# RetNet attention and a Swish MLP in one kernel: batch 1's queries loaded in two spans, the first MLP weights in half rows, the first up products in pairs

## The chip, the cores and the metric

The kernel runs on one core of one Trainium2 chip. The metric is the time of one execution on the device in microseconds (us): 311.66 us as the median of three runs (311.6 to 312.2). The profile is of one further execution. The engines are called as the profile calls them: PE multiplies matrices, DVE and POOL work elementwise, ACT does activations and copies, SP issues DMAs. PEld is PE's loading of the stationary operand, which lies beside its matmuls.

## The reference

`q`, `k` and `v` have 8 batches, 8 heads, 576 positions and 64 values per head. The output has 4608 rows of 512 values. Cut to what is computed:

```python
scores = scale * np.matmul(q, k.transpose(0, 1, 3, 2))
Dmat = np.where(rel >= 0, gamma[:, None, None] ** rel[None, :, :], 0.0)   # rel = i - j
attn_out = np.matmul(scores * Dmat[None], v)
x = attn_out.transpose(0, 2, 1, 3).reshape(B * S, H * D)                  # 4608 x 512
h = x @ w_in                                                              # 512 x 2048
g = h * (1.0 / (1.0 + np.exp(-beta * h)))
out = g @ w_out                                                           # 2048 x 512
```

There is no softmax: a fixed decay per head takes its place. So attention can be done in chunks of positions that hand on a state, the sum of keys times values.

## The kernel before, in words

**Work.** Each batch has 512 main positions in four chunks of 128; the last 64 positions of all batches are packed in a ninth block. Items of attention have a number i: i = 0 to 3 are the chunks of batch 0, 4 to 7 those of batch 1, 8 to 11 those of batch 2. For a chunk, keys become bf16 (`pre`, POOL), are turned by PE (`t_k`, four transposes, copied from PSUM by ACT, L304) and multiplied with the turned queries (`a_sc`); DVE multiplies the scores with the causal mask into `R` (L333, two products a chunk). `a_O` multiplies `R` with the values, `a_cross` adds queries times state, `a_x` copies the result into `xT`, the MLP's input (L380 to L384). `a_st` updates the state in PSUM and ACT copies it in two halves (L401), into `sbd`, or into `end` after the last chunk.

**Queries.** `pre_q` multiplies a batch's queries with gains (L247), `t_q` turns them in two groups of eight transposes (L297, L298). Before the change a batch's queries are laid out four positions to a partition, so every transpose needs all of the batch.

**MLP.** A block of 512 positions has 16 ups and 16 downs. An up (`up`, L406) is four matmuls, one for each quarter `ko` of the 512 inputs, into one of three PSUM tiles of the tag "mm", and a Silu on ACT (L415). A down is four matmuls of 512 columns (L426); four of them fill one output tile, which DVE copies (L433) and SP stores (L436).

**Order.** The order is written by hand. Batch 0's attention stands first, line by line (L457 to L497). Then `merged` goes through a list `fill` of MLP steps: 16 ups of batch 0 (steps 0 to 15), 16 downs (16 to 31, `d0` = 16), then batch 1 (`u1` = 32): ten ups of its first two chunks, ten of its last two, six whole ups, 16 downs, and so on. `streams` holds everything else with a key: a piece goes ahead of the first step whose number is not below its key. Each engine runs its instructions in this program order, so an instruction that waits holds up all that follows on its engine. At the same key order, `second` is `a_O`, `a_cross`, `a_x` of two chunks and the state of the second.

**Weights.** `w_in` comes through four staging tiles (tag "wt") and is cast to bf16 by DVE and POOL (L186). `w_out` comes through the same tiles, so its loads (L190) wait for these casts; it is scaled by DVE and ACT (L198, L200). SP issues nearly all DMAs in program order: batch 0's queries, keys and values, the pieces of `w_in`, those of `w_out`, then batch 1's queries, keys and values. A new load waits for one some eight places ahead of it, whose semaphore it takes.

Of the kernel before, what the change touches and what calls it, by code (L numbers as in the profile page):

```python
# [19 lines left out]
def kernel(  # L20
# [15 lines left out]
    P = 128  # L36
# [34 lines left out]
    QB = 2  # L71
    q_tiles, kv_tiles = {}, {}

    def load_q(b):
# [3 lines left out]
        t = stage.tile([P, H, CB, D], F32, name="qn", tag="qn", bufs=2)  # L78
        for u in range(2):
            w = slice(u * HP, (u + 1) * HP)  # L80
            nc.sync.dma_start(t[:, w].rearrange("p h i d -> p h (i d)"),
                              q[b, w, :MB, :].rearrange("h (p i) d -> p h (i d)", i=CB))
# [38 lines left out]
    pos = consts.tile([P, 2, CB + 1], F32, name="pos")  # L121
    for j, (step, mul) in enumerate(((1, CB), (P, 1))):
        nc.gpsimd.iota(pos[:, j, :CB], pattern=[[step, CB]], base=0, channel_multiplier=mul,
                       allow_small_or_imprecise_dtypes=True)
        for x in range(2):
            nc.gpsimd.iota(pos[x * TL:(x + 1) * TL, j, CB:], pattern=[[0, 1]], base=MB, channel_multiplier=1,
                           allow_small_or_imprecise_dtypes=True)
    lscale = consts.tile([P, 1], F32, name="lscale")
    nc.vector.memset(lscale[:], math.log(scale))
    lg = consts.tile([P, 2, CB + 1, H], F32, name="lg")  # L130
    for h in range(H):
        nc.vector.tensor_scalar(lg[:, :, :, h], pos[:], math.log(1.0 - 2.0 ** (-5.0 - h)), None, ALU.mult)
    gq = consts.tile([P, CB + 1, H], F32, name="gq")
    gv = consts.tile([P, CB + 1, H], F32, name="gv")
    nc.scalar.activation(gq[:], lg[:, 0], ACT.Exp, bias=lscale[:])
    nc.scalar.activation(gv[:], lg[:, 1], ACT.Exp, scale=-1.0)
# [11 lines left out]
    causal4 = consts.tile([P, HP, P], BF16, name="causal4")  # L148
    nc.gpsimd.tensor_copy(causal4[:], causal[:].unsqueeze(1).to_broadcast([P, HP, P]))
# [17 lines left out]
    pieces = [(f, 256) for f in range(0, 1024, 256)] + [(f, 512) for f in range(1024, d_ff, 512)]  # L167
# [5 lines left out]
    def load_w_in(g):  # L173
# [4 lines left out]
        nc.sync.dma_start(t, w_in_r[:, :, f0:f0 + fn])  # L178
        wts[g] = t

    def cast_w_in(g, kos=range(KO)):
        t = wts[g]
        f0, fn = pieces[g]
        for ko in kos:
            on_pool = ko == KO - 1 or g < 4 and ko > 1
            (nc.gpsimd if on_pool else nc.vector).tensor_copy(w_in_sb[:, ko, f0:f0 + fn], t[:, ko])  # L186
# [50 lines left out]
    def pre_q(b, n):  # L237
# [4 lines left out]
        if b < 2:  # L242
            hs, cs = slice(n // 2 * HP, (n // 2 + 1) * HP), slice(n % 2 * 2, n % 2 * 2 + 2)
            e = nc.vector
        else:
            hs, cs, e = slice(0, H), slice(n, n + 1), nc.gpsimd
        e.tensor_tensor(batch[b]["qs"][:, cs, hs], q_tiles[b][:, hs, cs].rearrange("p h i d -> p i h d"),  # L247
                        gq[:, cs, hs].unsqueeze(3).to_broadcast([P, cs.stop - cs.start, hs.stop - hs.start, D]),
# [50 lines left out]

    def t_k(i):  # L300
# [320 lines left out]
```

## Time and profile before

| what | value |
|---|---|
| median of three runs | 311.66 us |
| profiled execution | 311.92 us |
| its span, first to last instruction | 310.1 us |
| granted TensorE clock | 0.998 |
| first up of batch 0 | 19.48 us |
| first down of batch 0 | 34.12 us |
| first half up of batch 1 | 52.22 us |
| first down of batch 1 | 71.54 us |
| moved by DMA | 52.79 MB, 149 GB/s of HBM traffic over the span |

The page lists busy times of the engines, the span in 40 slices, the chain of work that ended last, and groups of instructions by line, with the time that their engine idled before them and what ended it. The timeline lists instructions in order of time: start, length, engine, line, operation, tiles, shape, number, and in brackets the idle time before and its releaser. Several alike are merged into one row, "x6". A busy time of PE counts a matmul from its start to the end of its pipeline, so waits on PE are read from the distances of starts. SPq and ACTq are the sequencers that issue DMAs.

### The profile page before, as it was taken

What the parts mean: (1) busy time and instruction counts of PE and PEld (TensorE: products, weight loads), DVE (VectorE), ACT (ScalarE), POOL (GpSimd) and SP (SyncE); (2) the same over time, 40 slices, a digit from 0 to 9 for tenths busy, and PEclk for the clock granted to TensorE, in tenths of its full rate; (3) what the DMA queues carried; (4) which work ended last, traced back from release to release, by engine and by line L of the source; (5) the groups of instructions that cost most, each with busy time, mean ns of one, the idle gap of its engine ahead of it and who ended that gap; (6) DMA issues with size and microseconds to landing.
All of it is one profiled execution on the core that took longest, in us unless ns stands there. A gap on an engine that the chain in (4) does not pass through costs nothing.

```text
span 310.1 us, 5363 instructions
## 1 busy us (share of the span) xinstructions
PE 298.5 (96%) x2144; PEld 157.8 (51%) x2177; DVE 106.9 (34%) x191; ACT 143.0 (46%) x256; POOL 96.0 (31%) x131
## 2 busy tenths in 40 slices
PE   7789999999999999999999999999999999999995
PEld 5544456775544454454554545455545444444444
DVE  7554476342531342434430434043405420010012
ACT  5567626995138412560186117711673037207700
POOL 4663026846524282254308031902420000000000
PEclk9999999999999999999999999999999999999999
DMA  8999999998989999999897697968852110031011
GB/s 207 221 355 387 380 232 273 233 257 179 202 197 162 224 189 235 218 212 198 133 234 107 136 205 207 201 115 192 196 76 37 68 70 0 17 88 34 0 70 68
DMA packets 123897, 52.79 MB, mean 170 GB/s; under 512 B 105680, under 2 KB 116320, under 8 KB 123872
## 3 DMA queue, kind: packets, MB, share of 16 engines
q1 hardware_dynamic: 98496, 46.15, 61.5%
q10 hardware_dynamic: 25376, 6.30, 13.6%
q8 instruction: 17, 0.28, 0.4%
q14 instruction: 8, 0.07, 0.1%
HBM read 36.71 MB, written 9.44 MB: 149 GB/s over the span
## 4 chain that ended last, share of the span: by engine, by line
PE 85%; DMA 6%; SPq 5%; DVE 1%; issue 1%; ACT 1%; POOL 1%; POOLq 0%
PE po L426 40%; PE ph L413 35%; DMA wt<-in_moe_w_in_dram 4%; SPq L94 3%; PE O L366 3%; PE sc L323 3%; DMA qn<-in_q_dram 2%; PE O L351 2%; PE st L396 2%; SPq L178 1%; POOL qs L247 1%; PE T L297 1%; PE T L303 1%; ACT gT L415 0%; DVE xT L384 0%
## 5 line engine op out<-in xcount | busy, mean ns | idle before, releaser
L415 ACT ACTIVATE gT<-ph,beta_sb 128x512 bf16<-128x512 f32 (+1 forms) x154 | 99.2, 659 | 86.3 <-PE ph L413 83.4
L413 PE MATMUL ph<-xT,w_in_sb 128*128 128x512 bf16 (+1 forms) x600 | 129.3, 365 | 3.2 <-DVE w_in_sb L186 0.9
L426 PE MATMUL po<-w_out_sb,gT 128*128 128x512 bf16 (+2 forms) x591 | 126.7, 368 | 1.1 <-issue 0.3
L413 PEld LDWEIGHTS <-w_in_sb 128*128 128x128 bf16 x616 | 58.7, 98 | 65.0 <-DVE w_in_sb L186 2.3
L426 PEld LDWEIGHTS <-gT 128*128 128x128 bf16 x608 | 57.1, 98 | 62.5
L333 DVE TENSOR_TENSOR R<-sc,causal 128x512 bf16<-128x512 f32 x71 | 44.3, 684 | 68.9 <-PE sc L323 68.9
L433 DVE COPY ot<-po 128x512 f32<-128x512 f32 (+2 forms) x38 | 25.0, 662 | 92.1 <-PE po L426 92.0
L255 POOL TENSOR_TENSOR vn<-kvn,gv 128x512 bf16<-128x512 f32 x32 | 33.4, 1042 | 22.8 <-DMA kvn<-in_v_dram 11.5
L247 POOL TENSOR_TENSOR qs<-qn,gq 128x512 bf16<-128x512 f32 x24 | 24.3, 1042 | 33.2 <-DMA qn<-in_q_dram 33.2
L273 POOL CAST kn<-kvn 128x512 bf16<-128x512 f32 x32 | 19.6, 612 | 47.7 <-DMA kvn<-in_k_dram 47.3
L401 ACT CAST sbd<-st 64x256 bf16<-64x256 f32 x48 | 17.4, 362 | 15.0 <-PE st L396 14.3
L384 DVE CAST xT<-O 128x512 bf16<-128x512 f32 x24 | 15.8, 688 | 19.6 <-PE O L366 9.6
L384 ACT CAST xT<-O 128x512 bf16<-128x512 f32 x11 | 6.4, 586 | 32.2 <-PE O L351 25.2
L396 PE MATMUL st<-vn,kn 128*128 128x128 bf16 x128 | 12.4, 219 | 0.2 <-POOL vn L255 0.2
L396 PEld LDWEIGHTS <-kn 128*128 128x128 bf16 x128 | 9.3, 98 | 5.0 <-issue 0.2
L366 PE MATMUL O<-R,vn 128*64 128x128 bf16 x288 | 10.7, 221 | 0.0
L323 PE MATMUL sc<-qT,kT 64*128 64x128 bf16 x256 | 10.3, 217 | 0.4 <-ACT kT L304 0.2
L366 PEld LDWEIGHTS <-vn 128*64 128x64 bf16 x288 | 8.5, 110 | 4.1 <-issue 3.6
L323 PEld LDWEIGHTS <-kT 64*128 64x128 bf16 x288 | 8.1, 94 | 3.8 <-ACT kT L304 1.5
L304 ACT COPY kT<-T 128x512 bf16<-128x512 bf16 x12 | 6.9, 586 | 4.8 <-PE T L303 4.8
L208 PE MATMUL ph<-warm 128*128 128x128 f32 (+1 forms) x24 | 7.0, 429 | 1.2 <-DVE warm L119 1.2
L186 DVE CAST w_in_sb<-wt 128x256 bf16<-128x256 f32 (+1 forms) x14 | 6.0, 476 | 5.2 <-DMA wt<-in_moe_w_in_dram 5.2
(56 smaller groups left out, 90.2 us busy)
## 6 DMA issues: line engine op xcount, KB each, us to landing
qn<-in_q_dram SPq DMA_DIRECT2D x16, 512.0 KB, 5.8
kvn<-in_k_dram SPq DMA_DIRECT2D x32, 256.0 KB, 5.9
kvn<-in_v_dram SPq DMA_DIRECT2D x32, 256.0 KB, 5.6
out_dram<-ot SPq DMA_DIRECT2D x31, 256.0 KB, 2.7
wt<-in_moe_w_out_dram SPq DMA_DIRECT2D x4, 1024.0 KB, 9.5
wt<-in_moe_w_in_dram SPq DMA_DIRECT2D x4, 512.0 KB, 7.5
wt<-in_moe_w_in_dram SPq DMA_DIRECT2D x2, 1024.0 KB, 11.8
out_dram<-ot SPq DMA_DIRECT2D x9, 128.0 KB, 2.4
```

The costliest lines, as they stand in the source:

```text
L247: e.tensor_tensor(batch[b]["qs"][:, cs, hs], q_tiles[b][:, hs, cs].rearrange("p h i d -> p i h d"), gq[:, cs, hs].unsqueeze(3).to_broadcas ...
L255: nc.gpsimd.tensor_tensor(live[i]["vn"][:], kv_tiles.pop(i)[:, 1], gains(gv, c), ALU.mult)
L273: nc.gpsimd.tensor_copy(kn[:, c % 2], t[:, 0])
L323: nc.tensor.matmul(view(sc[j][:, p, :]), L["kT"][r, p, :], rhs, start=True, stop=True, skip_group_check=True)
L333: nc.vector.tensor_tensor(R[:, j], sc[j][:], causal4[:] if i == CB - 1 else m_b, ALU.mult)
L366: nc.tensor.matmul(O[j * D:(j + 1) * D, p, :], vn[:, 2 * p + j, :], R[:, j, p, :], start=p == 0 and not (early and crossed), stop=early or ...
L384: (nc.scalar.copy if on_act else nc.vector.tensor_copy)(x, O[:])
L396: nc.tensor.matmul(st[:, p, :], heads(L["kn"], p), heads(L["vn"], p), start=(c == 0 and p == 0), stop=True, skip_group_check=True)
L413: nc.tensor.matmul(ph, w_in_sb[:, ko, fo * P:(fo + 1) * P], xts[m][:, ko, :, w], start=(ko == 0), stop=(ko == KO - 1))
L415: nc.scalar.activation(gts[m][:, fo, :, w], ph, ACT.Silu, scale=beta_sb[:, fo:fo + 1])
L426: nc.tensor.matmul(po[:, :nn], gT[:, fo, ms, :], w_out_sb[:, fo, n0:n0 + nn], start=(fo == 0), stop=(fo == FO - 1))
L433: nc.vector.tensor_copy(ot, po[:, :nn])
```

## The change

- **Weights.** `w_in` is cut into six pieces of 256 columns and one of 512 (before four and two). Each piece is loaded by two DMAs, `ko` 0 and 1, then 2 and 3. Its casts alternate between DVE and POOL; of piece 0, POOL and ACT do `ko` 0 and 1.
- **First ups.** Batch 0's ups go in pairs: `ko` 0 and 1 of both, then `ko` 2 and 3 of both, with the two Silus behind. The number of steps stays 16. The casts of `w_in` have new keys, and chunk 3's `a_st` goes behind the first step.
- **Batch 0's attention.** The copy `half` on ACT and the mask `causal4` are gone: both products of chunk 3 read PSUM. `a_x(1)` goes behind `t_k(3)`.
- **Batch 1's queries.** They lie in two spans of 256 positions, two positions to a partition, so a span's transposes need only that span. The first span is loaded ahead of the keys and values of chunks 4 and 5, the second behind these. They have a mask, gains and positions of their own (`causal_s`, `gs`). `t_span` turns a span; DVE and ACT each copy half of it.
- **Copies.** From i = 5 on, DVE copies odd chunks' keys in `t_k`; chunks 3, 5 and 7 have `xT` copied half by DVE and half by ACT.
- **Order.** The attention of batch 1 has new keys, and batch 2's stands two steps later at its start and one at its end.

```diff
+    def load_span(t, u):
+        nc.sync.dma_start(t[:, :, 2 * u:2 * u + 2].rearrange("p h i d -> p h (i d)"),
+                          q[SB, :, u * 2 * P:(u + 1) * 2 * P, :].rearrange("h (p i) d -> p h (i d)", i=2))
...
-    pieces = [(f, 256) for f in range(0, 1024, 256)] + [(f, 512) for f in range(1024, d_ff, 512)]
+    pieces = [(f, 256) for f in range(0, 1536, 256)] + [(f, 512) for f in range(1536, d_ff, 512)]
...
-        nc.sync.dma_start(t, w_in_r[:, :, f0:f0 + fn])
+        for u in range(2):
+            w = slice(u * KO // 2, (u + 1) * KO // 2)
+            nc.sync.dma_start(t[:, w], w_in_r[:, w, f0:f0 + fn])
...
-            on_pool = ko == KO - 1 or g < 4 and ko > 1
-            (nc.gpsimd if on_pool else nc.vector).tensor_copy(w_in_sb[:, ko, f0:f0 + fn], t[:, ko])
+            if g == 0 and ko == 1:
+                nc.scalar.copy(w_in_sb[:, ko, f0:f0 + fn], t[:, ko])
+            else:
+                on_pool = ko == 0 if g == 0 and ko < 2 else ko % 2
+                (nc.gpsimd if on_pool else nc.vector).tensor_copy(w_in_sb[:, ko, f0:f0 + fn], t[:, ko])
...
+    def t_span(u):
+        T = psum.tile([P, 2, HP, P], BF16, name="T", tag="mm" if u else "O", bufs=3 if u else 2)
+        for i in range(2):
+            for p in range(HP):
+                nc.tensor.transpose(T[:, i, p, :], heads(batch[SB]["qs"][:, 2 * u + i], p), ident[:])
+        nc.vector.tensor_copy(batch[SB]["qT"][:, 2 * u:2 * u + 1], T[:, :1])
+        nc.scalar.copy(batch[SB]["qT"][:, 2 * u + 1:2 * u + 2], T[:, 1:])
...
-        nc.scalar.copy(live[i]["kT"], T[:])
+        (nc.vector.tensor_copy if i > CB and i % 2 else nc.scalar.copy)(live[i]["kT"], T[:])
...
-        if i == CB - 1:
-            half = sb.tile([P, HP, P], BF16, name="half", tag="half", bufs=1)
-            nc.scalar.copy(half[:], sc[1][:])
-            sc[1] = half
         for j in range(2):
-            nc.vector.tensor_tensor(R[:, j], sc[j][:], causal4[:] if i == CB - 1 else m_b, ALU.mult)
+            nc.vector.tensor_tensor(R[:, j], sc[j][:], m_b, ALU.mult)
...
-        if i == CB - 1:
+        if i < 2 * CB and i % 2 and i != 1:
             nc.vector.tensor_copy(x[:, :2], O[:, :2])
             nc.scalar.copy(x[:, 2:], O[:, 2:])
...
+    def up_half(m, fo, u):
+        if m not in gts:
+            gts[m] = sb.tile([P, FO, CB, P], BF16, name="gT", tag="gT", bufs=2)
+        for f in (fo, fo + 1):
+            if u == 0:
+                phs[f] = psum.tile([P, MB], F32, name="ph", tag="mm", bufs=3)
+            for ko in range(u * KO // 2, (u + 1) * KO // 2):
+                nc.tensor.matmul(phs[f][:], w_in_sb[:, ko, f * P:(f + 1) * P], xts[m][:, ko],
+                                 start=(ko == 0), stop=(ko == KO - 1))
+            if u:
+                nc.scalar.activation(gts[m][:, f], phs[f][:], ACT.Silu, scale=beta_sb[:, f:f + 1])
...
-    fill = [F(up, 0, fo) for fo in range(FO)]
+    fill = [F(up_half, 0, fo, u) for fo in range(0, FO, 2) for u in range(2)]
...
-    streams = [[(0, F(load_w_out, 0)), (1.1, F(cast_w_in, 2)), (3.1, F(cast_w_in, 3)), (3.2, F(load_w_out, 1)),
-                (6.1, F(cast_w_in, 4)), (6.2, F(load_w_out, 2)), (10.1, F(cast_w_in, 5)), (10.2, F(load_w_out, 3))],
+    streams = [[(0, F(load_w_out, 0)), (0.05, F(a_st, 3)), (0.1, F(cast_w_in, 2)), (2.1, F(cast_w_in, 3)), (2.2, F(load_w_out, 1)),
+                (4.1, F(cast_w_in, 4)), (6.1, F(cast_w_in, 5)), (6.2, F(load_w_out, 2)), (8.1, F(cast_w_in, 6)),
+                (8.2, F(load_w_out, 3))],
                [(d0 - 4 + 3.3 * g, F(cast_w_out, g)) for g in range(WG)],
-               [(10.3, F(load_q, 1))] + [(10.3, F(load_kv, CB + n, (j,))) for n, j in keys_first],
+               [(10.3, F(load_q, 1))] + [(10.3 if n < 2 else 10.32, F(load_kv, CB + n, (j,))) for n, j in keys_first] + [(10.31, lambda: load_span(q_tiles[1], 1))],
...
-               [(d0 + 7, F(pre_q, 1, n)) for n in range(4)] + [(d0 + 10.6, F(t_q, 1, 0)), (d0 + 12.6, F(t_q, 1, 1))],
+               [(d0 + 7, F(pre_q, 1, 0)), (d0 + 7, F(pre_q, 1, 1)), (d0 + 12, F(t_span, 0)),
+                (d0 + 15.8, F(pre_q, 1, 3)), (u1, F(pre_q, 1, 2)), (u1 + 2, F(t_span, 1))],
...
-                (d0 + 12.7, F(t_k, 4)), (d0 + 12.8, F(t_k, 5)), (d0 + 13.8, F(a_sc, 4)), (d0 + 13.81, F(a_sc, 5)),
-                (d0 + 14.8, F(a_st, 4)), (d0 + 15.9, F(second, 4))],
+                (d0 + 13, F(t_k, 4)), (d0 + 14, F(t_k, 5)), (d0 + 14.1, F(a_sc, 4)), (d0 + 15, F(a_sc, 5)),
+                (d0 + 15.7, F(a_st, 4)), (d0 + 15.9, F(second, 4))],
...
-                (d0 + 15.8, F(t_k, 6)), (d0 + 15.91, F(t_k, 7)), (u1 + 1.8, F(a_sc, 6)), (u1 + 1.81, F(a_sc, 7)),
-                (u1 + 2.8, F(a_st, 6)), (u1 + 8.8, F(second, 6))]]
+                (u1 + 2.01, F(t_k, 6)), (u1 + 3, F(t_k, 7)), (u1 + 4, F(a_sc, 6)), (u1 + 4.01, F(a_sc, 7)),
+                (u1 + 5, F(a_st, 6)), (u1 + 9, F(second, 6))]]
...
-        lo, hi = (base[n] + 11, base[n + 1] - 12) if n == 1 else (base[n] + 3, base[n + 1] - 8)
+        lo, hi = (base[n] + 13, base[n + 1] - 11) if n == 1 else (base[n] + 3, base[n + 1] - 8)
```

## The prediction

> **What bounds the kernel now.** I read the page's busy times first, then its matmul groups, then the timeline stage by stage, and last the chain of waits.
>
> ```profile
> PE 298.5 (96%) x2144; PEld 157.8 (51%) x2177; DVE 106.9 (34%) x191; ACT 143.0 (46%) x256; POOL 96.0 (31%) x131
> ```
>
> PE is busy for 96% of the span. In the timeline 512-column matmuls start 0.216 us apart wherever nothing is awaited (the chain has 12 in 2.59 us), so a fill step of four takes 0.863 us, and four 256-column ones 0.437 us. A change can therefore gain only where PE waits. The table of stages shows where that is (columns: stretch, length, busy time of PE, PEld, DVE, ACT, POOL, clock, DMA share, GB/s):
>
> ```profile
> 0.00:19.90 19.90, 15.29 (x150) 10.63 (x152) 12.56 (x34) 11.82 (x24) 11.01 (x28) 1.00 1.09 242
> 19.90:34.12 14.22, 13.63 (x62) 6.08 (x65) 6.56 (x16) 10.93 (x17) 4.96 (x11) 1.00 1.05 383
> 34.12:52.22 18.10, 17.55 (x139) 9.55 (x140) 12.75 (x23) 7.10 (x14) 6.14 (x8) 1.00 1.08 275
> 52.22:71.54 19.32, 18.97 (x199) 14.04 (x201) 6.35 (x10) 17.47 (x39) 10.91 (x13) 1.00 1.08 260
> ```
>
> From 52.22 to 71.54 ACT is busy for 17.47 of 19.32 us: there it is nearly as full as PE. After 71.54 the change alters almost nothing. The waits of now are 0.61 us for weights at 26.6 to 27.3, and about 1.1 us around batch 1's attention (0.50 before 52.22, 0.33 before 56.07, 0.29 before 59.44, each the distance of two matmul starts less the stream's).
>
> ```profile
> 20.11 6.85 PE L413 MATMUL ph<-xT,w_in_sb 128*128 128x512 bf16 x31 [0.24 <-ACT end L401]
> 27.30 0.39 PE L413 MATMUL ph<-xT,w_in_sb 128*128 128x512 bf16 x1 [0.33 <-DVE w_in_sb L186]
> ```
>
> The second line is the wait for piece 4, the first with 512 columns.
>
> **1. Weights by halves, six pieces of 256.** The casts that waited for a DMA tell the landings: 18.85, 20.35, 21.85, 23.34 us for the 512 KB pieces (1.50 each, 1 KB rows), then 26.06, 28.77 and w_out's 31.49, 34.18, 36.89, 39.59 (2.71 per MB, 2 KB rows). The queue is backlogged throughout, so landings follow bytes and row length. After: halves land at about 18.1 and 18.85, pieces 4 and 5 at 24.85 and 26.35, the last at 29.06. The megabyte that goes from 2 KB to 1 KB rows costs 3.00 - 2.71 = 0.29 us; everything behind it lands that much later: w_out at 31.8, 34.5, 37.2, 39.9. SP issues eight DMAs more; at 0.55 us or less each (L178's rows) they are issued while megabytes are queued. Dearer than 0.1 us in all is unlikely; dearest would be 8 x 0.55 = 4.4 us if they stood alone.
>
> The Trainium skill speaks against the halves: "DMA: Bandwidth & Descriptors", section Bandwidth, asks for DMAs of 1 MiB or more and gives each a fixed part of about 2 us. Eight more would by that be up to 16 us if nothing overlapped (an estimate from that page); the 1.50 us between landings shows that it does overlap here.
>
> **2. First ups.** Now the first up matmul starts at 19.48 and the stream at 20.11, as if all had run from 19.89. After, ACT no longer copies `half` (0.58), so batch 0's last output comes some 0.25 us earlier: xT's DVE half at 18.34 to 18.76, ACT's at 18.80 to 19.17 (0.42 and 0.37, rows L380, L381; ACT waits for DVE). ACT then casts ko 1 until 19.5, so the second matmul runs at 19.65. The state update of chunk 3 (0.22), so far in idle time, now lies between. The pair's second ups wait for ACT: two `end` copies (0.37 each), then Silu at 21.45 to 22.14; fo 3 takes fo 0's PSUM tile (three of them) and starts at 22.2 instead of 21.8. Pair 2 starts at 23.50; up 4 now starts at 19.89 + 16 x 0.216 = 23.34. So the head is 0.16 worse, and without the 0.61 wait the ups would end at 23.50 + 6 x 1.727 = 33.86, against 34.12 now. That is the gain on offer: 0.26 us.
>
> **3. ACT takes it back.** The key of w_out's first cast is unchanged: fill step 12.
>
> ```profile
> 31.53 0.72 ACT L198 ACTIVATE w_out_sb<-wt,rbeta_sb 128x512 bf16<-128x512 f32 x1
> 32.16 1.98 ACT L415 ACTIVATE gT<-ph,beta_sb 128x512 bf16<-128x512 f32 x3
> 34.12 0.59 PE L426 MATMUL po<-w_out_sb,gT 128*128 128x512 bf16 x2
> ```
>
> Now ACT sits at that cast until the data lands; single ups have two tiles in hand and PE feels nothing. In pairs there is no such reserve: fo 15 needs fo 12's tile. Cast at 31.9 (landing 31.8), Silu 12 at 32.53 to 33.22, fo 15 from 33.27, six matmuls more: downs start at **34.56, +0.44**. This holds whatever the head gains. Bounds: 33.86 (-0.26) if w_out lands by 31.1, +0.8 if it lands 0.35 later still. I take +0.44.
>
> **4. Batch 1's queries by spans.** A span is 512 KB in 512-byte rows, of which the trace has next to none. Nearest rows: 256-byte rows run at 219 GB/s (stretch 6 to 14 us), 1 KB at 349 (512 KB in 1.50). So a span takes 1.5 to 2.4 us; between them, by time per packet (18.8 and 46.4 ns per engine), 28 ns x 64 = 1.8. It lands at 41.7, its keys at 42.9 and 44.0, its values at 45.2 and 46.4. Its gains (0.69 on DVE, 1.04 on POOL beside it) are done by 42.8. The transposes stand at step 28, 34.56 + 12 x 0.863 = 44.9. Cover 2.1 us, so the order of loads is worth nothing and 2.4 us would cost nothing. "DMA: Bandwidth & Descriptors", section Specifications, puts line rate at 512 bytes and up; by that a span takes 1.5 us and the sum is the same.
>
> **5. Chunks 4 and 5.** Now:
>
> ```profile
> 47.64 0.62 PE L323 MATMUL sc<-qT,kT 64*128 64x128 bf16 x16
> 48.42 0.81 PE L426 MATMUL po<-w_out_sb,gT 128*128 128x512 bf16 x3 [0.16 <-issue]
> 49.29 1.03 PE L426 MATMUL po<-w_out_sb,gT 128*128 128x512 bf16 x4
> 50.47 0.64 PE L366 MATMUL O<-R,vn 128*64 128x128 bf16 x16
> 52.22 0.83 PE L413 MATMUL ph<-xT,w_in_sb 128*128 128x256 bf16 x6 [0.34 <-DVE xT L384]
> ```
> ```profile
> 48.07 2.48 DVE L333 TENSOR_TENSOR R<-sc,causal 128x512 bf16<-128x512 f32 x4 [0.94 <-PE sc L323]
> 50.47 0.68 DVE L433 COPY ot<-po 128x512 f32<-128x512 f32 x1
> 51.47 0.69 DVE L384 CAST xT<-O 128x512 bf16<-128x512 f32 x1 [0.32 <-PE O L351]
> ```
>
> DVE's four mask products begin 0.43 us after the first score; the third ends 2.31 and the fourth 2.91 after it. Between scores and outputs PE has two steps of downs and key transposes, so the outputs come 2.83 later, just in time. After, the scores stand at step 31 and the outputs at 32: one step. By PE: 34.56 + 15 x 0.863 + 0.89 of transposes = 48.40; scores 0.56, a step 0.87 and a switch 0.1, state 0.22: 50.1. The outputs need the tiles that chunk 5's scores hold: 50.76 (wait 0.6), second half 51.36 (wait 0.3), cross until 51.9. Then xT: DVE half 52.1 to 52.53, ACT half to 52.95. First up at 52.58, its third matmul at 53.0: as if from **52.78** (now 52.22). By then PE has done 0.90 us less (second half of the query transposes, 0.45; transposes of keys 6 and 7, 0.45).
>
> **6. Half ups.** PE's work from there to batch 1's downs: now 19.32 with about 0.8 of waits; after 0.90 more. The waits, ACT in program order: Silu 0.47 (0.37 apart when queued), keys' copy 0.58, state 0.75. ACT has xT until 52.95, state until 53.73; Silu 0 and 1 until 54.57; half of the queries' copy until 55.08; Silu 2; keys 6 at 55.37 to 55.95. PE is ready for chunk 6's scores at 55.57: wait 0.43. Waits for PSUM tiles before halves 2 and 8: 0.15 and 0.19. Outputs at 59.36; xT of chunk 7 in two halves (DVE to 61.01, ACT to 61.42): wait 0.2; `end` copies until 62.18, Silu 9 until 62.65, whose tile half 12 needs at 62.13: wait 0.57. In sum 1.54. Half 12 starts at 62.7, now at 60.33: **+2.4**. What follows is the same on both sides (now 11.21 to the downs; I reckon 11.1 to 11.2). ACT's relief (keys 5, 7 and half the queries on DVE: 0.58 + 0.58 + 0.43) is used up by xT halves that wait for DVE and by order.
>
> Causal masks, gains and one more iota before 5 us: POOL and DVE have 0.28 us to spare before the queries land; over that, it costs its own size, 0.1. The rest of the run shifts as a whole; the 0.77 us wait at 164 us hangs on an output's copy and moves along (from 0 to 0.8).
>
> **Sum.** 0.44 to the downs, 0.12 to the first half up, 1.8 in the halves: +2.3 after rounding down 0.06. The profiled execution took 311.92 us (span 310.1); it stands 0.26 over the median 311.66, so 314.2 there and **314.0** against the median.
>
> **Rivals.**
> - *Relief outruns the waits* (faster). Place: 48 to 63 us. The 1.12 us of waits of now go, none comes, the 0.44 stays: -0.68, 311.0. It decides if PE comes to chunk 4's outputs 2.4 us or more after its scores and ACT copies keys 6 before PE wants them. For it: ACT is the fuller engine there. Against: one step of 0.87 instead of two. 0.14.
> - *ACT never holds PE* (no change): downs at 33.86 and no waits in the halves: 2.3 - 0.7 - 1.54 = +0.1, 311.8. Needs w_out by 31.1; bytes speak against. 0.14.
> - *As forecast*: 312.6 to 315.2. 0.62.
> - *Data is late too*: from 16 us on the slowest DMA ring runs about 1.4 us behind the others, after a fetch of 16 KB of instructions on it (1.42 us in the DMA records); a second one on that ring before 30 us puts the downs at 35.9: 315.4 and over. 0.10.
>
> That the queries' order does nothing holds in all four. A measurement tells about 0.2% (0.62 us) from no change; faster 0.14, same 0.14, slower 0.72. The range takes in the no-change case and most of the forecast's: 311.0 to 315.4, leaving out most of the faster case and the last.
>
> **What would show it.** Right: ups without a gap at 26 us; ACT's w_out cast between Silu 11 and 12 and a gap before fo 15; downs at 34.5; waits at L366 behind L333 near 50.5; half 12 near 62.7. Wrong: downs before 34.0, or R finished before the outputs, or PE ahead of now at 60 us.

## The result, and the profile after

The changed kernel takes **314.91 us** (median; 314.19 to 315.69), the kernel before 311.63 (311.6 to 312.2) beside it: a ratio of 1.0096 [1.0079, 1.0113], so it is slower by 3.3 us. In a second comparison it was 314.1 against 311.38, 1.0075 [1.0052, 1.0098], 2.7 us. The forecast was 314.0, its range 311.0 to 315.4. The profiled execution of after took 314.19 us, its span 312.5; against the profiled execution of before that is 2.27 more (311.92, span 310.1).

Page of after, busy times. The 33 matmuls more are records that the trace of before lacks, not work, so PE's busy sums are not to be compared; the distances of starts are.

```profile
PE 301.7 (97%) x2177; PEld 158.0 (51%) x2177; DVE 106.6 (34%) x193; ACT 141.3 (45%) x256; POOL 101.4 (32%) x139
```

The table of stages of after, cut at the first up, the first down, the first half up and batch 1's first down (columns as in the prediction):

```profile
0.00:19.17 19.17, 14.54 (x146) 10.33 (x146) 12.16 (x33) 10.83 (x22) 10.76 (x30) 1.00 1.08 235
19.17:34.64 15.47, 14.89 (x68) 6.42 (x69) 5.46 (x17) 10.98 (x20) 7.77 (x16) 1.00 1.06 374
34.64:52.82 18.18, 17.14 (x126) 8.83 (x124) 11.79 (x22) 5.51 (x11) 7.87 (x9) 1.00 1.12 263
52.82:74.45 21.63, 20.59 (x217) 14.86 (x218) 8.07 (x14) 18.36 (x41) 13.14 (x16) 1.00 1.11 259
```

| start of | before | after | late by |
|---|---|---|---|
| first down, batch 0 | 34.12 | 34.64 | 0.52 |
| first half up, batch 1 | 52.22 | 52.82 | 0.60 |
| first down, batch 1 | 71.54 | 74.45 | 2.91 |
| last matmul | 306.60 | 309.26 | 2.66 |
| end of the span | 310.14 | 312.47 | 2.33 |

Of the 2.91 us at batch 1's downs, 0.52 come ahead of the first down, only 0.08 between there and the half ups, and 2.31 in the stage of half ups, where ACT is busy for 18.36 of 21.63 us. But 0.90 us of PE's transposes moved from the second of these stretches into the third (half of the queries', and those of keys 6 and 7), so by waits the second is about 1.0 worse than before and the third about 1.4. The clock is 1.00 in every stage.

**From the ups to the downs.** Timeline of after, PE, ACT and DVE:

```profile
19.17 0.38 PE L458 MATMUL ph<-xT,w_in_sb 128*128 128x512 bf16 x1 [0.63 <-DVE xT L412]
19.79 0.82 PE L458 MATMUL ph<-xT,w_in_sb 128*128 128x512 bf16 x3 [0.24 <-ACT w_in_sb L205]
...
22.38 12.43 PE L458 MATMUL ph<-xT,w_in_sb 128*128 128x512 bf16 x54 [0.25 <-ACT gT L461]
...
32.00 0.72 ACT L220 ACTIVATE w_out_sb<-wt,rbeta_sb 128x512 bf16<-128x512 f32 x1
32.01 1.28 DVE L222 TENSOR_SCALAR w_out_sb<-wt,rbeta_sb 128x512 bf16<-128x512 f32 x3 [2.36 <-DMA wt<-in_moe_w_out_dram]
32.63 1.25 ACT L461 ACTIVATE gT<-ph,beta_sb 128x512 bf16<-128x512 f32 x2
34.64 1.67 PE L472 MATMUL po<-w_out_sb,gT 128*128 128x512 bf16 x7
```

The wait for weights at 26 to 27 us is gone. In its place ACT's cast of `w_out` begins when DVE's does, at the landing (32.0), and only then come Silu 12 and 13 (32.63); by the distances of starts PE loses 0.25 us at 33.35 for a tile, and 0.08 in each of the five pairs ahead of it. In before the cast stood in the same place, but single ups had tiles in hand.

**Chunks 4 and 5.** Timeline of after, DVE and PE:

```profile
49.62 1.88 DVE L365 TENSOR_TENSOR R<-sc,causal_s 128x512 bf16<-128x512 f32 x3
50.95 0.41 PE L398 MATMUL O<-R,vn 128*64 128x128 bf16 x8 [0.56 <-DVE R L365]
51.55 0.41 PE L398 MATMUL O<-R,vn 128*64 128x128 bf16 x8 [0.18 <-DVE R L365]
52.82 1.22 PE L444 MATMUL ph<-xT,w_in_sb 128*128 128x256 bf16 x8 [0.30 <-DVE xT L412]
```

In before these 16 output matmuls were one row with no wait. Now PE stands twice for DVE's mask products; by the distances of starts it loses 0.72 and 0.37 us, then 0.46 for `xT`.

**Half ups.** Timeline of after, DVE, ACT and PE:

```profile
54.51 0.42 DVE L331 COPY qT<-T 128x512 bf16<-128x512 bf16 x1 [0.98 <-PE T L330]
54.97 0.58 ACT L332 COPY qT<-T 128x512 bf16<-128x512 bf16 x1 [0.29 <-DVE qT L331]
55.82 0.59 ACT L338 COPY kT<-T 128x512 bf16<-128x512 bf16 x1
56.47 0.40 PE L360 MATMUL sc<-qT,kT 64*128 64x128 bf16 x8 [0.62 <-ACT kT L338]
61.67 0.37 ACT L413 CAST xT<-O 128x256 bf16<-128x256 f32 x1
61.94 0.74 ACT L433 CAST end<-st 64x256 bf16<-64x256 f32 x2
62.71 1.63 ACT L446 ACTIVATE gT<-ph,beta_sb 128x256 bf16<-128x256 f32 x4
63.24 1.03 PE L444 MATMUL ph<-xT,w_in_sb 128*128 128x256 bf16 x8 [0.32 <-ACT gT L446]
```

ACT's half of the query copy starts only when DVE's half is done; keys 6 stand behind it and behind a Silu, and PE waits for them (0.78 us). At 63.24 PE waits for a PSUM tile whose Silu stood behind ACT's half of `xT` and the two `end` copies (0.49).

### The profile page after: what moved, and what is told of

It is laid out like the page before. It is cut to its first block, busy times and chain, and to the rows that moved or that the text cites. A ratio compares the mean times of both kernels' runs of the same rounds, so it can differ in the third digit from the quotient of the medians.

```text
span 312.5 us, 5418 instructions
## 1 busy us (share of the span) xinstructions
PE 301.7 (97%) x2177; PEld 158.0 (51%) x2177; DVE 106.6 (34%) x193; ACT 141.3 (45%) x256; POOL 101.4 (32%) x139
## 4 chain that ended last, share of the span: by engine, by line
PE 82%; DMA 7%; SPq 5%; ACT 2%; DVE 2%; POOL 1%; issue 1%; ACTq 0%; POOLq 0%
PE po L472 40%; PE ph L444 32%; SPq L105 3%; DMA wt<-in_moe_w_out_dram 3%; PE sc L360 3%; PE O L398 3%; DMA wt<-in_moe_w_in_dram 2%; DMA qn<-in_q_dram 2%; PE O L383 2%; PE st L428 2%; SPq L197 1%; DVE R L365 1%; POOL qs L273 1%; ACT gT L446 1%; PE ph L458 0%
## 5 line engine op out<-in xcount | busy, mean ns | idle before, releaser
L472 PE MATMUL po<-w_out_sb,gT 128*128 128x512 bf16 (+2 forms) x608 | 129.0, 368 | 0.0
L446 ACT ACTIVATE gT<-ph,beta_sb 128x512 bf16<-128x512 f32 (+1 forms) x138 | 88.4, 656 | 82.6 <-PE ph L444 79.3
L444 PE MATMUL ph<-xT,w_in_sb 128*128 128x512 bf16 (+1 forms) x552 | 116.6, 364 | 1.2 <-ACT gT L446 0.8
L365 DVE TENSOR_TENSOR R<-sc,causal 128x512 bf16<-128x512 f32 x64 | 39.9, 684 | 66.2 <-PE sc L360 66.2
L416 DVE CAST xT<-O 128x512 bf16<-128x512 f32 x22 | 14.5, 688 | 17.5 <-PE O L398 10.5
L458 PE MATMUL ph<-xT,w_in_sb 128*128 128x512 bf16 x64 | 15.0, 378 | 1.2 <-DVE xT L412 0.6
L461 ACT ACTIVATE gT<-ph,beta_sb 128x512 bf16<-128x512 f32 x16 | 10.1, 682 | 3.2 <-PE ph L458 3.2
```

Of the source, the lines that this page charges most:

```text
L365: nc.vector.tensor_tensor(R[:, j], sc[j][:], m_b, ALU.mult)
L416: (nc.scalar.copy if on_act else nc.vector.tensor_copy)(x, O[:])
L444: nc.tensor.matmul(ph[:, :cn], w_in_sb[:, ko, fo * P:(fo + 1) * P], xts[m][:, ko, c0:c0 + cn], start=(ko == 0), stop=(ko == KO - 1))
L446: nc.scalar.activation(gts[m][:, fo, c0:c0 + cn], ph[:, :cn], ACT.Silu, scale=beta_sb[:, fo:fo + 1])
L458: nc.tensor.matmul(phs[f][:], w_in_sb[:, ko, f * P:(f + 1) * P], xts[m][:, ko], start=(ko == 0), stop=(ko == KO - 1))
L472: nc.tensor.matmul(po[:, :nn], gT[:, fo, ms, :], w_out_sb[:, fo, n0:n0 + nn], start=(fo == 0), stop=(fo == FO - 1))
```

## The experiments

All times are medians; "before" is the kernel before on the same chip, in the same comparison. The first four share one comparison (before: 311.38), the next four another (311.47), then three (311.63) and one (311.37). A shift of 0.2 to 0.4 us between two kernels can be the landing of `w_out` alone, since the downs of after hang on it: in two profiles of the changed kernel `w_out` landed at 32.00 and 32.35, and the first down stood at 34.64 and 34.99.

**r1, the changed kernel again.** No edit.

> The changed kernel once more, as the measure for the others: the four executions so far spread from 314.19 to 315.69 us, where the kernel before keeps within 0.6. If its waits are those of program order alone (theory), its profile has the first down of batch 0 at 34.6 us, the first half up of batch 1 at 52.8 and batch 1's first down at 74.4 again, whatever the execution's time. If a landing sets one of them (rival: data comes late), that stage moves with the weights' or queries' landing from profile to profile, by up to 1.5 us. 314.2 to 315.7.

314.1 (313.49 to 314.55), ratio 1.0075 [1.0052, 1.0098]. Theory and rival each hold in part: the first down came at 34.99, 0.35 later, with `w_out`'s landing, while the stages behind it lasted as long as in after (18.17 and 21.72 us, against 18.17 and 21.63).

**r2, single ups.**

```diff
-    fill = [F(up_half, 0, fo, u) for fo in range(0, FO, 2) for u in range(2)]
+    fill = [F(up, 0, fo) for fo in range(FO)]
```

> The change with batch 0's ups one at a time again (the halves of the loads stay). Theory (ACT and the PSUM tiles hold the pairs): the waits of 0.41 at fo 3 and 0.08 in each pair go; Silu 12 still stands behind w_out's first cast on ACT (ending at 33.3), and up 15 needs its tile, so the downs start at 34.2 instead of 34.64: 0.4 faster than the change. Rival (the halved loads and their landings cost it): downs stay at 34.6, no gain.

313.65 (313.35 to 314.1): 0.45 under r1, as expected. First down at 34.11, where it was before the change, and a wait of 0.76 us in front of up 15 for the Silu behind the cast. So pairs cost what was reckoned, and single ups alone don't bring a gain over the kernel before. In this profile the half ups took 21.98 us: DVE's product for the second span took 1.48 us beside a product of POOL's (0.86 in after), and PE waited 0.34 us for it.

**r3, single ups, and DVE casts the first quarter that ACT cast.**

```diff
-            if i == KO - 1:
+            if i == KO - 1 and g > 0:
```

> As r2, and the last quarter of w_out's first group is scaled by DVE instead of ACT. Theory: with ACT free Silu 12 is not held, the downs start at 33.6, which is 1.0 earlier than in the change and 0.5 earlier than before the change; the time is 1.0 below the change's. Rival (w_out's landing at 31.9 itself is the bound, not ACT's place in the queue): four casts on DVE end at 33.7, downs at 34.2 as in r2.

313.11 (312.23 to 313.58): 1.0 under r1, as expected. First down at 33.36, with no wait of PE from 20 to 46 us. The weights part is worth 0.76 us at the first down (34.12 before) if ACT doesn't sit at a DMA.

**r4, chunk 4's and 5's scores one step earlier** (pairs kept).

```diff
-                (d0 + 13, F(t_k, 4)), (d0 + 14, F(t_k, 5)), (d0 + 14.1, F(a_sc, 4)), (d0 + 15, F(a_sc, 5)),
+                (d0 + 12, F(t_k, 4)), (d0 + 13, F(t_k, 5)), (d0 + 13.1, F(a_sc, 4)), (d0 + 14, F(a_sc, 5)),
...
-(d0 + 12, F(t_span, 0)),
+(d0 + 11, F(t_span, 0)),
```

> The change with the query and key transposes and the scores of chunks 4 and 5 one step earlier, so that two steps of downs lie between scores and outputs, as before the change. Theory (PE waits for DVE's four mask products): the waits of 0.72 and 0.37 us before the outputs go, the first half up of batch 1 starts at 51.8 instead of 52.8; 1.0 faster than the change. Rival (keys or values are late, so the earlier transposes wait instead): PE waits at the key transposes near 46.5, nothing gained.

313.09 (312.55 to 314.52), 1.0 under r1, but the mechanism gave less. Timeline of r4, PE:

```profile
50.06 0.78 PE L398 MATMUL O<-R,vn 128*64 128x128 bf16 x16
51.03 0.40 PE L383 MATMUL O<-qT,sbd 128*128 128x128 bf16 x4 [0.20 <-ACT sbd L433]
```

The two waits for `R` are gone, the outputs are one row again; a wait for ACT's copy of chunk 4's state (0.37 us by starts) is new. From the first down to the first half up it takes 17.57 us, in after and r1 18.17: 0.6 won. Besides, the first down of this profile is at 34.38 instead of r1's 34.99, which is the landing and not the edit.

**r5, keys of chunk 6 copied by DVE** (pairs kept).

```diff
-        (nc.vector.tensor_copy if i > CB and i % 2 else nc.scalar.copy)(live[i]["kT"], T[:])
+        (nc.vector.tensor_copy if i > CB and i % 2 or i == CB + 2 else nc.scalar.copy)(live[i]["kT"], T[:])
```

> The change with the copy of chunk 6's turned keys on DVE, which idles there. Theory (ACT's queue holds PE in the half ups): the wait of 0.78 before chunk 6's scores shrinks to 0.1, and ACT, 0.58 lighter, shortens the tile waits of 0.25, 0.17 and 0.49 that follow; from the first half up of batch 1 to its first down 20.6 instead of 21.63; 0.8 to 1.2 faster than the change. Rival (PE itself is full there, 0.9 of transposes having moved in): the wait only moves on, under 0.3 gained.

313.58 (313.06 to 314.11): 0.5 under r1, less than expected. The wait in front of chunk 6's scores fell from 0.78 to about 0.2 and the stage from 21.63 to 21.18; the later waits (0.25, 0.17, 0.49) stood as they were. That wait did not hide them, nor they it.

**r6, the spans alone**: the changed kernel with the weights, casts, ups and chunk 3's state of before.

```diff
-    pieces = [(f, 256) for f in range(0, 1536, 256)] + [(f, 512) for f in range(1536, d_ff, 512)]
+    pieces = [(f, 256) for f in range(0, 1024, 256)] + [(f, 512) for f in range(1024, d_ff, 512)]
...
-        for u in range(2):
-            w = slice(u * KO // 2, (u + 1) * KO // 2)
-            nc.sync.dma_start(t[:, w], w_in_r[:, w, f0:f0 + fn])
+        nc.sync.dma_start(t, w_in_r[:, :, f0:f0 + fn])
...
-    fill = [F(up_half, 0, fo, u) for fo in range(0, FO, 2) for u in range(2)]
+    fill = [F(up, 0, fo) for fo in range(FO)]
...
```

> The kernel before with the spans of batch 1 and all else of the change except the weights: pieces, loads, casts, single ups and chunk 3's state are as before. Theory (two thirds and more of the loss lie in batch 1's order): downs of batch 0 at 34.1 as before, first half up 18.2 later, first down of batch 1 at 73.9, so 2.3 slower than before. Rival (the head's halves and pairs are the loss, and batch 1 only inherits their delay): within 0.6 of before.

313.85 (313.24 to 315.12), ratio 1.008 [1.0059, 1.0101]: 2.4 over before, as expected. Downs at 34.10, first half up at 52.27, batch 1's downs at 73.90 (71.54 before). So of the 2.9 us at that point the spans and their order bring 2.4.

**r7, the weights alone**: the kernel before with the weights part, single ups, and r3's cast.

```diff
-    pieces = [(f, 256) for f in range(0, 1024, 256)] + [(f, 512) for f in range(1024, d_ff, 512)]
+    pieces = [(f, 256) for f in range(0, 1536, 256)] + [(f, 512) for f in range(1536, d_ff, 512)]
...
-        nc.sync.dma_start(t, w_in_r[:, :, f0:f0 + fn])
+        for u in range(2):
+            w = slice(u * KO // 2, (u + 1) * KO // 2)
+            nc.sync.dma_start(t[:, w], w_in_r[:, w, f0:f0 + fn])
...
-            if i == KO - 1:
+            if i == KO - 1 and g > 0:
...
```

> The kernel before with the change's weights alone: six pieces of 256 columns by halves and their casts, but single ups, w_out's first group scaled by DVE alone, and batch 1 as before. Theory: no wait at 26 us and none for Silu 12; downs of batch 0 at 33.4 instead of 34.1, and batch 1's data, 0.3 later, is still early: 0.7 faster than before, 310.7. Rival (the megabyte in 1 KB rows delays batch 1's queries and keys): the gain is lost at batch 1's transposes, within 0.2 of before.

311.94 (310.85 to 313.06), ratio 1.0017 [1.0003, 1.0031]: a miss, no gain, if anything a small loss. The first down came at 33.37 as reckoned, batch 1's first at 71.30 only, 0.24 ahead of before; behind that this profile lost 1.49 us to waits that are the subject of the next section (0.89 in before). Timeline of r7, DVE and PE:

```profile
42.74 1.29 DVE L252 TENSOR_TENSOR qs<-qn,gq 128x512 bf16<-128x512 f32 x2 [0.28 <-DMA qn<-in_q_dram]
43.95 1.88 DVE L438 COPY ot<-po 128x512 f32<-128x512 f32 x3
44.69 1.02 PE L431 MATMUL po<-w_out_sb,gT 128*128 128x512 bf16 x4 [0.35 <-DVE ot L438]
```

DVE waits for the queries' DMA (42.74); its copies of finished outputs stand behind, and PE has no PSUM tile: 0.52 us lost by starts. The queries land no earlier than in before (41.17 and 42.74, there 41.09 and 42.66), so earlier downs run into them.

**r8, everything mended**: the changed kernel with the edits of r2 to r5 and chunk 4's state one step earlier.

```diff
-                (d0 + 15.7, F(a_st, 4)), (d0 + 15.9, F(second, 4))],
+                (d0 + 14.7, F(a_st, 4)), (d0 + 15.9, F(second, 4))],
```

> The change with all of it mended: single ups, w_out's first group scaled by DVE, transposes and scores of chunks 4 and 5 and chunk 4's state one step earlier (r4 left a wait of 0.36 for that state), chunk 6's keys copied by DVE. Theory: downs at 33.4, first half up at 50.6, first down of batch 1 at 71.2 to 71.8: 0.3 faster than before to 0.3 slower. Rival (something in the spans that was not found costs more): 1 or more slower than before.

312.52 (312.27 to 313.16), ratio 1.004 [1.0024, 1.0055]: 1.05 over before, a miss. First down at 33.36, batch 1's at 72.57. With the downs early, the query transposes stand for their product (0.71 us by starts, at 43.57), and the later waits of the half ups stay (0.25, 0.17 and 0.49). The repairs add up to 1.9 of the 2.9 us; the spans don't reach the old time.

**r9, r7 with the second two query products on POOL.**

```diff
-            e = nc.vector
+            e = nc.gpsimd if b == 1 and n > 1 else nc.vector
...
-(d0 + 12.6, F(t_q, 1, 1))],
+(d0 + 13.6, F(t_q, 1, 1))],
```

> The kernel before with the weights by halves in six pieces of 256, single ups and w_out's first cast on DVE, as in the earlier run of the weights alone; now the second two of batch 1's four query products are on POOL instead of DVE, and the second group of query transposes stands one step of downs later (13.6 instead of 12.6 steps behind the first down). Theory: in the earlier run PE lost 0.515 us at step 28 because the copies of the outputs stood behind the query products on DVE, and these waited for their data; then that loss goes, batch 1's downs start at 70.8 (71.30 in the run of the weights alone, 71.54 in the kernel before) and the time is 0.5 to 0.8 us under the kernel before, if the wait near 125 us is not larger than 0.4. Rival: the loss is due to the data itself, which lands when it lands; then the wait goes to the query transposes or to the scores of chunk 4, downs of batch 1 at 71.3 and the time within 0.3 us of the kernel before.

312.32 (311.33 to 313.57), ratio 1.0029 [1.0013, 1.0046]: a miss. Batch 1's downs at 73.05, 1.75 later than in r7. Timeline of r9, POOL and PE:

```profile
43.54 2.04 POOL L252 TENSOR_TENSOR qs<-qn,gq 128x512 bf16<-128x512 f32 x2 [13.02 <-DMA qn<-in_q_dram]
45.53 1.17 POOL L278 CAST kn<-kvn 128x512 bf16<-128x512 f32 x2
46.20 0.40 PE L308 MATMUL T<-ident,kn 128*128 128x128 bf16 x4 [0.79 <-POOL kn L278]
```

The copies of the outputs are free (no wait at step 28), so the cause named for r7 holds; but now chunk 4's and 5's keys stand behind the products on POOL, and the scores behind late query transposes. In this profile the weights and queries also landed some 0.8 later than in that of r7 (41.94 against 41.17), so up to 0.8 of the 1.75 is not the edit's. In r7 DVE's products stand at the landing itself: what limits them is when the queries land.

**r10, r9 with the later batches' keys turned by SP.** Ten of the 24 DMA transposes (`x_k`) are issued by SP instead of ACT.

```diff
-    def turn(dst, src):
-        nc.scalar.dma_start_transpose(...)
+    def turn(dst, src, e=nc.scalar):
+        e.dma_start_transpose(...)
...
-        turn(kT, kn)
+        turn(kT, kn, nc.sync)
```

> The run with the second two query products on POOL, and besides the later batches' keys are turned by DMA transposes that SP issues instead of ACT. Theory: near 123 to 129 us ACT takes 1.9 to 3.5 us to issue one such transpose and its Silus stand behind it, so PE lost 0 to 1.37 us there from run to run; on SP the wait near 125 us goes in every run, the five times lie closer together and the mean is 0.3 to 0.8 us lower than with ACT issuing. Rival: SP's other work (loads and output stores stand behind the transposes there, which wait for POOL's casts) is delayed and the loss comes back as a wait for output tiles or for keys; then the time is the same or higher.

311.71 (311.5 to 311.88 over 11 runs), ratio 1.0001 [0.9991, 1.0011]: 0.6 under r9, as expected, and the spread shrank from 2.24 to 0.38 us. What this settles is shown below, at the wait of 164 us.

**r11, chunks 5 and 7 copied whole**: after with `xT` of these chunks on DVE alone.

```diff
-        if i < 2 * CB and i % 2 and i != 1:
+        if i == CB - 1:
...
-            on_act = i < 2 * E or b is not None and c == 1
+            on_act = i < E or i % 2 == 0 if i < 2 * E else b is not None and c == 1
```

> The changed kernel, with one part undone: the attention results of chunks 5 and 7 are copied whole by DVE (0.69 us) while ACT copies those of chunks 4 and 6, as in the kernel before; chunk 3 stays in halves. Theory: the halves do not run side by side, ACT waits for DVE's half, so whole copies cost the first half up 0.25 us and give back the 0.17 us wait of its third matmul, and they free ACT 0.37 us earlier twice: the wait at 62.6 us goes from 0.49 to about 0.12 and the one of 0.17 at 61.8 goes; in all the stage of half ups is 0.4 to 0.6 us shorter and the time 0.3 to 0.6 us under the changed kernel's 314.1. Rival: halves are faster because both engines share one copy: then undoing them costs 0.2 to 0.3 us at each of the two chunks, and the time is 0.4 us over the changed kernel's.

314.54 (313.27 to 315.06), not under the changed kernel's: a miss. The stage of half ups was 21.26 us instead of 21.63, and the wait in front of half 12 went from 0.49 to none. But the first half up now waits for a whole copy. Timeline of r11, PE:

```profile
52.92 1.05 PE L444 MATMUL ph<-xT,w_in_sb 128*128 128x256 bf16 x8 [0.56 <-DVE xT L416]
```

By starts that is 0.72 us, 0.46 in after, so the stage ahead is 0.27 longer (18.44 instead of 18.17), and of the 0.37 only 0.10 is left at batch 1's downs. A wait of 1.16 us at 168 us in its profile (0.63 in after) took more than that; it is the one of the next section.

**r12, r7 with the keys turned by SP**: the edits of r7 and of `turn` in r10.

> The kernel before with the weights by halves in six pieces of 256, single ups and w_out's first cast on DVE (as in the run of the weights alone, all four query products on DVE), and the later batches' keys turned by DMA transposes that SP issues. Theory: the downs of batch 1 start at 71.3 as in the run of the weights alone, and the waits near 125 us (0.12 in the kernel before, 1.13 in that run) and near 164 us (0.77 and 0.36) go, because both come from ACT's issue of such a transpose, behind which its Silus stand; then the span is 308.7, the time 310.2 to 310.6, 1.0 to 1.4 us under the kernel before, and the runs lie within 0.5 us. Rival: the waits near 125 and 164 us come from the output's copies or from loads and stay, or SP's stores suffer; then the time is 311.2 or more, as in the run with the queries on POOL and the turns on SP.

311.02 (310.78 to 311.45), ratio 0.9989 [0.9978, 1.0001]: 0.35 us under before, which this doesn't tell from no change. One half of the expectation held, the waits at 125 and 164 us are gone; the other didn't: the wait for the query products was 0.90 instead of 0.52 us, for the downs stood 0.14 earlier and the queries landed 0.25 later, so batch 1's downs came at 71.56. The runs spread over 0.67 us (before: 310.69 to 312.76). No version here is clearly faster than the kernel before.

## Why the prediction was right, and where its terms were off

**1. Weights.** Right: landings followed bytes and row length. `w_out` landed at 32.0 (31.8 reckoned; 31.3 to 32.4 over the profiles with these weights), the wait at 26 to 27 us went, and the eight DMAs more cost nothing that shows. Their price was misread: 0.54 us was the least of L178's six issues, the median 0.75, the longest 2.80. The fixed part of about 2 us stands in the Trainium skill, "DMA: Bandwidth & Descriptors", not in section Bandwidth but in Anatomy of one DMA — SWDGE (gpsimd) path, for DMAs that POOL issues. Here SP issues them, and 256 KB halves landed 0.75 us apart. With single ups and the cast on DVE, r7 and r3 reach 0.75 us at the first down.

**2. First ups.** In the profile of after `xT`'s DVE half started at 18.60 (18.34 reckoned, 18.59 before), but there the scores of chunk 3 themselves were late, the last at 16.39; in r1, the same kernel, it came at 16.04. Timeline of r1, DVE:

```profile
18.25 0.42 DVE L412 CAST xT<-O 128x256 bf16<-128x256 f32 x1 [0.66 <-PE O L398]
```

From the last score to this row it is 2.20 or 2.21 us in after, r1 to r6, r8 and r11, and 2.38 or 2.39 in before, r7, r9, r10 and r12, which keep `half`: taking it out brought 0.2 of the 0.25 reckoned. The wait of some 0.4 at the second ups was 0.41. The head of now was misread: counted back from the first down, 20.11 is the third matmul, the second being one of the records that the trace of before lacks, so its stream ran as if from 19.68 and not 19.89. The reckoned head was thus 0.37 worse than it, not 0.16; the times that the prediction goes on with stand. What it left out is that pairs lose 0.08 us each for PSUM tiles even where ACT isn't held. In after this didn't count at the downs, for ACT's cast came later still. In r5, where `w_out` landed at 31.28 and the cast followed Silu 11 at once, it did: the downs came at 34.01, where the lower bound had been 33.86.

**3. ACT's cast.** Right: downs at 34.64 (34.56 reckoned). In after, r1, r4 and r11, the profiles with pairs in which the cast waited, the first down stands 2.64 us behind the landing (32.00, 32.35, 31.74 and 31.84). In before ACT didn't sit there, as the prediction read it: the cast began at 31.53, as Silu 11 ended. r2 and r3 take the two halves of the reason apart: the pairs' missing reserve is worth 0.5 us, the cast on ACT 0.75 more (first downs at 34.64, 34.11 and 33.36).

**4. Spans.** Right: their order is worth nothing here. The queries were at 41.97, the transposes at 45.00 without a wait. The product on DVE took longer than reckoned:

```profile
41.97 1.57 DVE L273 TENSOR_TENSOR qs<-qn,gs 128x512 bf16<-128x512 f32 x1 [0.59 <-DMA qn<-in_q_dram]
```

1.57 us beside POOL's 1.04 (41.96 to 43.00), against 0.69 for the same with POOL idle in before (and 0.68 in r4 at 51.81, where DVE began 0.14 ahead of POOL). The Trainium skill, "SBUF — State Buffer", section SBUF: two separate sides, says that a DVE operation with two inputs in SBUF and a POOL operation that reads SBUF exclude each other for a whole instruction, and that the one that starts first goes through; POOL began 0.01 us ahead and took its usual 1.04, DVE ended 0.54 after POOL's end, so the trace agrees. The span itself took 1.86 us (from the last piece of `w_out` at 40.11 to 41.97; 1.8 reckoned), 512 KB of 1 KB rows 1.50. "DMA: Bandwidth & Descriptors", section Specifications, has line rate from 512 bytes up; here 512 KB in rows of 512 bytes took a quarter longer than in rows of 1 KB.

**5. Chunks 4 and 5.** Right in kind and nearly in size: 0.72 and 0.37 us at the outputs (0.6 and 0.3 reckoned). The first half up started at 52.82 (52.58 reckoned), and its third matmul lost 0.17 for ACT's half of `xT` (0.2): as if from 52.99, against 52.78. r4 shows that it is the one step between scores and outputs.

**6. Half ups.** Here a term was mis-sized. The wait in front of chunk 6's scores was to be 0.43 and was 0.78: the query copy was reckoned as two halves side by side, done at 55.08, but ACT's half waits for DVE's and ended at 55.56. The other waits came to 0, 0.25, 0.17 and 0.49 (0.15, 0.19, 0.2, 0.57 reckoned), 1.69 in all instead of 1.54, and two gaps of some 0.1 lie beside the scores, which stand apart now. With the 0.21 of the stage ahead half 12 starts at 63.24 instead of 62.7. After that 11.21 us to the downs, as reckoned: they are 2.91 late instead of 2.4. r6 gives the spans' share without the weights: 2.4.

**The rest of the run.** The step that failed: "the 0.77 us wait at 164 us hangs on an output's copy and moves along". It hangs on ACT. Timeline of before, ACT and its DMA sequencer (ACTq), and PE:

```profile
162.09 0.69 ACT L415 ACTIVATE gT<-ph,beta_sb 128x512 bf16<-128x512 f32 x1 [0.18 <-PE ph L413]
162.17 2.29 ACTq L281 DMA_TRANSPOSE kT<-kn  x1
164.50 2.49 ACT L415 ACTIVATE gT<-ph,beta_sb 128x512 bf16<-128x512 f32 x4 [1.73 <-POOL qs L247]
165.24 2.10 PE L413 MATMUL ph<-xT,w_in_sb 128*128 128x512 bf16 x9 [0.60 <-ACT gT L415]
```

ACT spends 2.29 us on issuing one DMA transpose; the next Silus stand behind it and PE runs out of PSUM tiles. The bracket at 164.50 names POOL, whose second `qs` product ended at 164.46, when the issue did. But a Silu doesn't read `qs`, and in after the two come apart: the product ended at 166.93, the issue at 167.11, and the Silu started at 167.16. The same transpose at 123 us did the same. The length of the issue differs from execution to execution, and what PE loses is that length less a reserve (us):

| profile | issue near 163 | PE loses | issue near 125 | PE loses |
|---|---|---|---|---|
| before | 2.29 | 0.77 | 2.32 | 0.12 |
| after | 2.15 | 0.63 | 1.87 | 0 |
| r2 | 1.25 | 0 | 2.57 | 0.39 |
| r6 | 1.25 | 0 | 3.55 | 1.37 |
| r7 | 1.88 | 0.36 | 3.34 | 1.13 |
| r9 | 2.00 | 0.48 | 2.19 | 0 |
| r11 | 2.68 | 1.16 | 1.97 | 0 |

Near 163 the loss is the issue less 1.52 in every row that has one, near 125 the issue less 2.2. The profiles that the table leaves out follow this too: r1 lost 0.52 of 2.04, r3 0.64 of 2.16 and 0.27 of 2.46, r5 0.57 of 2.09, r8 0.72 of 2.24, r4 nothing that shows. Timeline of r6, ACT and PE, the dearest case:

```profile
125.56 3.55 ACTq L302 DMA_TRANSPOSE kT<-kn  x1
129.16 2.49 ACT L441 ACTIVATE gT<-ph,beta_sb 128x512 bf16<-128x512 f32 x4 [2.75 <-PE ph L439]
129.89 1.46 PE L439 MATMUL ph<-xT,w_in_sb 128*128 128x512 bf16 x6 [1.20 <-ACT gT L441]
```

With SP as issuer ACT goes on with its Silus every 0.86 us and PE loses nothing at either place. A row from the timeline of r12, ACT:

```profile
125.52 0.69 ACT L420 ACTIVATE gT<-ph,beta_sb 128x512 bf16<-128x512 f32 x1 [0.18 <-PE ph L418]
```

So a wait that was to move along as a constant costs 0 to 1.5 us from one profile to the next, over the twelve in which ACT issues these transposes. Before has one profile among them (0.89), after two (0.63 and 0.52). Taking it off ACT narrowed the runs from 2.24 to 0.38 us (r9, r10) and from 2.21 to 0.67 (r7, r12). It does not make the change's 2.3 to 3.3 us.

**Why 2.3 in the profiles and up to 3.3 in the medians.** In the profiles: 2.91 at batch 1's downs, less 0.26 at the two places above, less 0.33 at the tail, from the last matmul to the end. Neither of the two belongs to the change: the first is the length of the issue, and the tail is 3.2 us in after, r9 and r10, but 3.5 to 3.7 in before, r6, r7 and r12, whichever code they have. So that the profiles differ by 2.27 where 2.3 was forecast is in part luck: the sum was 0.5 short at batch 1's downs, and 0.6 came back by chance behind them. The profiled execution of before lay 0.3 to 0.5 us above its medians (311.92 against 311.63 and 311.38), that of after 0.7 below its first median (314.19 against 314.91). After's own landing of `w_out` moved its downs from 34.64 to 34.99 between two profiles. Single ups in before would not feel 0.35 (Silu 12 ended at 32.83, and up 15, which needs its tile, started at 33.26), though no run shows before with a later landing. Whether these two make up the whole difference between 2.7 and 3.3 was not measured.

**The rivals.** *Relief outruns the waits* needed outputs behind finished `R` and keys 6 copied in time; the rows above show waits at both. *ACT never holds PE* needed `w_out` by 31.1 and no waits in the half ups; neither came. *Data is late too* did not come as a second lag in after. The first one, though, sets the landing of `w_out` and not the bytes alone. A DMA adds to its semaphore in sixteen parts: from 14.5 to 16.2 us the last of these comes at most 0.21 us behind the one before it, in every profile, and from 17.2 us on it hangs behind, in after by 1.3 us up to `w_out` (fifteen parts by 30.61, the last at 31.92), in r5 by 1.0, in r1 by 2.1 at first. Over after and its variants the landing moved between 31.3 and 32.35. So in after all but one part of `w_out` had come ahead of the 31.1 of the rival before; what the downs would gain without the lag no run shows.

## What to carry to other kernels

A wait that is taken away ahead of a stage brings only what the next data allows: here the weights part won 0.75 us and lost 0.52 of it again (r7), ten microseconds later, to queries that landed when they always had. An engine that copies from PSUM should not stand at a DMA, be it a load's cast or the issue of a transpose, for the PSUM tiles that are free meanwhile are all the reserve that PE has. A copy split over two engines is worth its two halves only if they start together. In this program order the second waited for the first, so the split brought the first half up 0.27 us forward and cost 0.37 behind it. And where a forecast agrees with a single profile to a tenth of a microsecond, waits that change from execution to execution are worth a look before the sum is believed.

## What the runs showed of the hardware

- ACT issued 316 DMA transposes in the fourteen profiles: 226 of them held it for 1.25 to 1.4 us, 66 for more than 1.85, up to 3.63 (r2 at 83.33). Beside 58 of the 66 SP was issuing a load, but it was so beside 76 of the 226 as well; what makes an issue long was not found. SP's own issues are long at times too (2.1 us for two query loads in before at 123.15, 4.5 for a load in r6 at 129.30). On SP in r12 such a transpose took 1.25 at 126.70 and 4.64 at 157.80, and PE lost nothing there.
- r10 and r12 issue ten key transposes from SP while ACT still issues those of the queries and four of the keys'. The Trainium skill, "DMA: Bandwidth & Descriptors", section DMA Transpose (X-bar), warns that transposes of two queues in flight together can spoil each other's data. No run here was made to show that; whoever keeps the edit moves all of them to one queue, or makes one wait for the other. That wasn't tried.
- DVE and POOL products with both inputs in SBUF, begun together, ended at 43.54 and 43.00: DVE's took more than twice its 0.69 us.
- From about 17 us on one of a DMA's sixteen parts lands 1.0 to 2.1 us behind most of the others, in thirteen of the fourteen profiles (in r11 0.6 to 0.8, with a second late one). It begins about when 16 KB of instructions are fetched: that fetch starts at 15.3 to 16.25 us and takes 1.0 to 1.6 (1133 ns in after, 1467 in r1). In the twelve profiles with the change's weights `w_out` landed 14.6 to 14.9 us after the end of this fetch, between 31.28 and 32.40. Whether the fetch holds that part up, or both follow something else, no run shows.
